# Linear attention with a beta-swish layer: where in GpSimd's queue the copy of v for batch 3 stands

## The chip, the cores and the metric

The kernel runs on one core of a Trainium2 chip. The metric is the device time of one execution in microseconds (us), as the median of several runs. Times inside an execution come from its hardware trace and count from the start of its span.

## What is computed

Two layers follow one another. First comes linear attention over 8 batches of 8 heads, 576 tokens and 64 numbers per head. Then comes a two-layer network on the 4608 tokens of 512 numbers, with a hidden width of 2048:

```python
def phi(x):                       # on q and k
    return np.where(x > 0, x, np.exp(x) - 1.0) + 1.0
kv  = np.einsum('bhsd,bhse->bhde', phi(k), v)
z   = np.sum(phi(k), axis=2)
num = np.einsum('bhsd,bhde->bhse', phi(q), kv)
den = np.einsum('bhsd,bhd->bhs', phi(q), z)[..., None] + 1e-06
x   = num / den                   # then (batch, token, head * 64)
h   = x @ w_in                    # 512 -> 2048
g   = h * (1.0 / (1.0 + np.exp(-beta * h)))
out = g @ w_out                   # 2048 -> 512
```

## The kernel before

The 576 tokens of a batch are read as 64 groups of 9. The first 8 tokens of all groups give four tiles of 128 tokens, which are the network's work of that batch, 512 tokens. The ninth tokens of all 8 batches are collected in `xT_tail` and make a ninth piece of work of the same size. So there are nine passes of the network. Each has a first half H (`h_phase`: 16 groups of 4 TensorE matmuls of 128x128 by 128x512, each followed by a swish on ScalarE, L454 and L462) and a second half Y (`y_phase`: 4 output tiles with 16 such matmuls each, L472, then a copy of the tile by VectorE, L245, and its way out by DMA). In this text, H2 and Y1 are the H half of pass 2 and the Y half of pass 1.

The attention of later batches is threaded in between. `manual_schedule` keeps every engine's instructions in the order in which the program writes them, and an engine takes its own in that order. The main loop (L838 to L871) writes pass b and keeps two lists of side work, `sh` for H and `sy` for Y: `at(sy, 5, f)` writes f behind the matmuls of group 5 of that Y half (group 4t + i is quarter i of output tile t). The number thus places the work in the queue of every engine that f uses. It is not a time: an engine that has nothing else to do takes its next instruction as soon as what it waits for is there, even when TensorE is still far from that group.

What a batch m needs, in the order of its data:

- q, k and v come by DMA. `load_q` and `load_k` are issued from GpSimd's queue, `load_v` from SyncE's for batches from 3 on. `load_q(m+1, after)` is held (`hold`, L88) until the DMA transposition of phi(q) of batch m has landed. It stands in GpSimd's queue in front of `load_k(m+2)` (L863, L864).
- phi(q) and phi(k): exp on ScalarE (L144), the positive part (L148) and a minimum (L155) on VectorE.
- phi(q) is transposed by DMA into `qTd` (L275), issued from SyncE.
- v is copied by GpSimd in two instructions (`v_copies`, L516; the copy is L173) from float32 `vf` to bfloat16 `vaug`, of which there are two, for even and odd batches. The column behind each 64 numbers of `vaug` was set to one at the start (L113), so that one matmul with phi(k) gives kv and z together.
- kv of batch m: `kv_pair` (L230) makes 36 small matmuls of 64x64 by 64x65 for half of the heads, L184. For batch 3 both halves are written in H2 by `kv_both(3)` behind group 8, right behind `odd_numers` (16 small matmuls, L356, for the ninth tokens of batches 0 and 1). For batches from 4 on they are the first matmuls of `numers` (L322) behind the last group of H.
- `numers(n, m)` makes the numerators and denominators of batch n (L309), and VectorE divides (L383 to L404). Then `x_trans_dma` (L439, issued from SyncE, L442) transposes them into `xT`, the input of H of pass n.

What stands around the change, in the pass b = 1 (n = 2, m = 3): `load_v(3)` behind group 2 of H1. In Y1, `numers(2)` behind group 1, the transpositions of batch 2's x behind groups 2 and 3, phi(q) of batch 3 behind group 3. Then:

```python
at(sy, 5, lambda: q_trans_dma(m), lambda: load_q(m + 1, st[m, "qTd", "dma"]))
at(sy, 5, lambda: load_k(m + 2))
if b == 1:
    at(sy, 8, lambda: phi_all(3, "k"), lambda: v_copies(3))
at(sy, 9, lambda: load_v(m + 1))
```

So GpSimd's queue held, in this order: the load of q of batch 3 and those of k of batches 3 and 4, the load of q of batch 4 (held), the load of k of batch 5, the copies of v of batch 3, and the copies of v of batch 4 (written in H2 behind group 6).

Of the kernel before, what the change touches and what calls it, by code (L numbers as in the profile page):

```python
# [16 lines left out]
def kernel(  # L17
# [153 lines left out]
    def v_copy(eng, b, pr):  # L171
        src = vb[b % 2] if b == 2 else vf[b % 2]
        eng.tensor_copy(  # L173
            vaug[b % 2][:, pr, :, :, 0:D], src[:, places(b, pr)].rearrange("p h j d -> p j h d")
        )
# [51 lines left out]
    def num_tile(name):  # L227
        return numps.tile([P, 2, 512], F32, tag="num", name=name)
# [4 lines left out]
    def kv_both(b):  # L233

        t = num_tile("kvp")
        for pr in range(2):
            kv_pair(b, pr, [t[:, hh, pr * EA : (pr + 1) * EA] for hh in range(2)])
        st[b, "kvd"] = work.tile([P, 2, 2 * EA], BF16, tag="kv_bd", name="kvd")
        nc.vector.tensor_copy(st[b, "kvd"], t[:, :, 0 : 2 * EA])
# [32 lines left out]
    def q_trans_dma(b):  # L272
        st[b, "qTd"] = work.tile([P, 4 * J, G], BF16, tag="qT", name="qTd")
        for hh in range(2):
            st[b, "qTd", "dma"] = nc.sync.dma_start_transpose(  # L275
                out=st[b, "qTd"][:, hh * 2 * J : (hh + 1) * 2 * J],
                in_=st[b, "q"][hh * G : (hh + 1) * G].rearrange("p a j c -> p (a j c)"),
            )

    def q_odd_trans(b, tp):  # L280

        tv = tp.rearrange("p (a n) -> p a n", a=2)
        for pr in range(2):
            nc.tensor.matmul(
                tv[:, pr], st[b, "q"][:, pr, J - 1, :], identity,
                is_transpose=True, start=True, stop=True, skip_group_check=True,
            )
        nc.scalar.copy(
            q_odd[b].rearrange("p (i a) g -> p a i g", i=2),
            tv.rearrange("p a (i g) -> p a i g", i=2),  # L290
        )
# [30 lines left out]
    def numers(b, after=None):  # L322

        pairs = [num_tile("nps") for _ in range(2)]
        odd = [mm_tile("nps_m") for _ in range(2)]
        if after is not None:
            for pr in range(2):
                kv_pair(after, pr, [pairs[pr][:, hh, 6 * EA : 7 * EA] for hh in range(2)])
        for k in range(2):
            dst = [pairs[k][:, h] for h in range(2)]  # L330
            numer_tile(b, dst, k)
            numer_tile(b, dst, 2, (k,), 4)
        numer_tile(b, odd, 3)
        for hh in range(2):
            quads(b, odd, 4 + hh, lambda c: (c, J - 1), hh, None)
        st[b, "nps"] = pairs, odd
        for k in range(3):
            norms(b, k)
        if after is not None:
            st[after, "kvd"] = work.tile([P, 2, 2 * EA], BF16, tag="kv_bd", name="kvd")  # L340
            for pr in range(2):
                nc.vector.tensor_copy(
                    st[after, "kvd"][:, :, pr * EA : (pr + 1) * EA],
                    pairs[pr][:, :, 6 * EA : 7 * EA],
                )
# [93 lines left out]
    def x_trans_dma(b, t):  # L439
        xv = st[b, "xs", t].rearrange("p n d -> p (n d)")  # L440
        if t < NT - 1:
            nc.sync.dma_start_transpose(out=x_dst(b, t), in_=xv)  # L442
            return

        for pr in range(2):
            nc.sync.dma_start_transpose(
                out=xT_tail[:, places(b, pr), b * G : (b + 1) * G],
                in_=xv[pr * G : (pr + 1) * G, 0 : 2 * P],
            )
# [39 lines left out]
    def load_q(b, after):  # L489
        if b < B:  # L490
            hold(load(nc.gpsimd, xq[b % NX], q, b), after)

    def load_k(b):
        if b < B:
            load(nc.gpsimd, xk[b % NX], k, b)

    def load_v(b):
        if b < B:
            load(nc.sync, vf[b % 2], v, b)

    def phi_exps(b, a):
        for pr in range(2):
            phi_part(b, a, pr, xin(b, a, pr))

    def phi_rest(b, a):
        phi_tile(b, a)
        for pr in range(2):
            phi_relu(b, a, pr, xin(b, a, pr))
        for pr in range(2):
            phi_min(b, a, pr)  # L510

    def phi_all(b, a):
        phi_exps(b, a)
        phi_rest(b, a)

    def v_copies(b):  # L516
        for pr in range(2):
            v_copy(nc.gpsimd, b, pr)
# [284 lines left out]
    def h_phase(b, x, side):  # L803
        for ff in range(FC):

            if b == 1 and ff in (3, 4):
                hp = num_tile("h_ps2")[:, 0]
            else:
                hp = mm_tile("h_ps")
            h_mm(b, x, ff, hp)  # L810
            silu(b, ff, hp)
            run(side, ff)

    def y_phase(b, side, last=False):
        for t in range(4):
            if last and t == 3:
                for c0, c1 in ((0, 320), (320, 512)):
                    yp = mm_tile("y_ps")
                    for i in range(4):
                        y_mm(b, t, i, yp, c0, c1)  # L820
                    y_out(b, t, yp, c0, c1, (nc.sync, nc.scalar))
                break
            yp = mm_tile("y_ps")
            halves = ((0, 256), (256, 512)) if b == 1 and t > 1 else ((0, 512),)
            for cols in halves:
                for i in range(4):
                    y_mm(b, t, i, yp, *cols)
                    if i < 3 and cols is halves[-1]:
                        run(side, 4 * t + i)
            y_out(b, t, yp)  # L830
            run(side, 4 * t + 3)

    def at(side, n, *fs):
        side.setdefault(n, []).extend(fs)
# [3 lines left out]
    for b in range(1, B + 1):  # L838
        n = b + 1
        m = n + 1  # L840
        sh, sy = {}, {}
        if b == 1:
            at(sh, 0, lambda: q_trans_dma(2))
            at(sh, 1, lambda: v_copies(2))
            at(sh, 2, lambda: load_q(3, st[2, "qTd", "dma"]), lambda: load_k(3))
            at(sh, 2, lambda: load_v(3), lambda: load_k(4))
            at(sh, 6, lambda: q_odd_trans(1, num_tile("qop")[:, 0].bitcast(BF16)[:, 0:256]))
            at(sh, 8, lambda: kv_both(2))
            at(sy, 1, lambda: numers(2))
        elif n < B:  # L850
            if b == 2:
                at(sh, 8, odd_numers, odd_norms, lambda: kv_both(3))
                at(sh, 9, lambda: [x_trans_dma(i, 4) for i in range(2)])
            if m < B:
                at(sh, 2, lambda: phi_rest(m, "k"))
                at(sh, 6, lambda: v_copies(m))
            at(sh, FC - 1, lambda: numers(n, m if m < B else None))
        if n < B:
            for t in range(NT):
                at(sy, t // 3 + (2 if b == 1 else 0), lambda t=t: x_trans_dma(n, t))  # L860
        if m < B:
            at(sy, 3, lambda: phi_all(m, "q"))
            at(sy, 5, lambda: q_trans_dma(m), lambda: load_q(m + 1, st[m, "qTd", "dma"]))  # L863
            at(sy, 5, lambda: load_k(m + 2))  # L864
            if b == 1:
                at(sy, 8, lambda: phi_all(3, "k"), lambda: v_copies(3))
            at(sy, 9, lambda: load_v(m + 1))
            if m + 1 < B:
                at(sy, 10, lambda: phi_exps(m + 1, "k"))
        h_phase(b, xT[b % 3] if b < B else xT_tail, sh)  # L870
        y_phase(b, sy, last=(b == B))  # L871
# [30 lines left out]
```

## Time and profile before

| what | before |
|---|---|
| time, median of 3 runs | 286.87 us (286.58 to 286.91) |
| span of the profiled execution | 285.2 us |
| granted TensorE clock | 0.999 |
| TensorE matmul busy | 274.3 us, 96% |
| ScalarE busy | 160.7 us, 56% |
| VectorE busy | 106.4 us, 37% |
| GpSimd busy | 37.1 us, 13% |
| DMA, mean over the span | 144 GB/s |

How to read it: PE is TensorE and PEld its loading of weights, which runs beside the matmuls; DVE is VectorE, ACT ScalarE, POOL GpSimd, SP SyncE. A q behind a name means the queue that issues (POOLq, SPq). L173 is line 173 of the kernel. A row in order of time gives the start, the duration, the engine, the line, the operation and what it wrote from what, and in square brackets how long the engine had been idle and what ended that. Matmuls overlap, so the busy time of a row is from its first start to its last end, and the ends of matmuls are modelled; intervals between starts are the better measure.

### The profile page before, as it was taken

What the parts mean: (1) busy time and instruction counts of PE and PEld (TensorE: products, weight loads), DVE (VectorE), ACT (ScalarE), POOL (GpSimd) and SP (SyncE); (2) the same over time, 40 slices, a digit from 0 to 9 for tenths busy, and PEclk for the clock granted to TensorE, in tenths of its full rate; (3) what the DMA queues carried; (4) which work ended last, traced back from release to release, by engine and by line L of the source; (5) the groups of instructions that cost most, each with busy time, mean ns of one, the idle gap of its engine ahead of it and who ended that gap; (6) DMA issues with size and microseconds to landing.
All of it is one profiled execution on the core that took longest, in us unless ns stands there. A gap on an engine that the chain in (4) does not pass through costs nothing.

```text
span 285.2 us, 5976 instructions
## 1 busy us (share of the span) xinstructions
PE 274.3 (96%) x2477; PEld 139.0 (49%) x2508; DVE 106.4 (37%) x260; ACT 160.7 (56%) x219; POOL 37.1 (13%) x51
## 2 busy tenths in 40 slices
PE   7799999999997999999999999999999999999994
PEld 2584457454844544454445444544444444444443
DVE  5842677706732464037403740281025100110012
ACT  5778587974784842885288617831860186028500
POOL 8732100320007001300041002100000000000000
PEclk9999999999999999999999999999999999999999
DMA  7999999679999928963997369336303410230033
GB/s 217 205 213 391 248 262 186 150 202 230 186 133 280 153 65 186 291 109 66 151 273 141 81 152 271 63 80 147 88 3 79 114 39 0 57 80 12 0 74 75
DMA packets 51723, 41.03 MB, mean 144 GB/s; under 512 B 31584, under 2 KB 43120, under 8 KB 51696
## 3 DMA queue, kind: packets, MB, share of 16 engines
q1 hardware_dynamic: 38800, 23.61, 35.0%
q0 software_dynamic: 12736, 16.91, 30.5%
q8 instruction: 19, 0.31, 0.5%
q10 hardware_dynamic: 160, 0.13, 0.2%
q14 instruction: 8, 0.07, 0.1%
HBM read 36.71 MB, written 9.44 MB: 162 GB/s over the span
## 4 chain that ended last, share of the span: by engine, by line
PE 90%; DMA 4%; issue 1%; ACT 1%; POOL 1%; DVE 1%; SPq 0%; POOLq 0%
PE y_ps L472 43%; PE h_ps L454 40%; DMA xk<-in_k_dram 2%; DMA qTd<-phi_q 2%; PE nps L184 1%; PE h_ps L665 1%; PE nps L309 1%; ACT e L144 1%; POOL vaug L173 1%; PE kvp L184 1%; DVE phi_k L155 1%; PE nps_m L309 0%; PE nps L631 0%; PE tp L655 0%; PE nps L563 0%
## 5 line engine op out<-in xcount | busy, mean ns | idle before, releaser
L462 ACT ACTIVATE g<-h_ps,beta_c 128x512 bf16<-128x512 f32 x144 | 97.8, 689 | 89.2 <-PE h_ps L454 88.7
L472 PE MATMUL y_ps<-w_out,g 128*128 128x512 bf16 (+3 forms) x615 | 125.9, 360 | 1.0 <-issue 0.2
L454 PE MATMUL h_ps<-xT,w_in 128*128 128x512 bf16 x487 | 108.5, 379 | 0.8 <-ACT e L144 0.3
L472 PEld LDWEIGHTS <-g 128*128 128x128 bf16 x632 | 60.8, 98 | 61.1
L454 PEld LDWEIGHTS <-w_in 128*128 128x128 bf16 x560 | 54.4, 98 | 65.6 <-DVE y_sb L245 0.7
L245 DVE COPY y_sb<-y_ps 128x512 f32<-128x512 f32 (+2 forms) x37 | 24.8, 675 | 82.5 <-PE y_ps L472 81.4
L392 DVE TENSOR_SCALAR den<-nps 128x12 f32<-128x12 f32 x12 | 2.0, 166 | 63.5 <-PE nps L309 63.5
L144 ACT ACTIVATE e<-xk 128x1152 bf16<-128x1152 bf16 x16 | 17.8, 1153 | 3.2 <-DVE phi_k L155 1.6
L83 POOL DMA_DIRECT2D xq<-in_q_dram x7 | 5.2, 746 | 95.0 <-DMA qTd<-phi_q 49.7
L144 ACT ACTIVATE e<-xq 128x1152 bf16<-128x1152 bf16 x14 | 15.6, 1155 | 1.4 <-DMA xq<-in_q_dram 1.3
L454 PE MATMUL h_ps<-xT_tail,w_in 128*128 128x512 bf16 x62 | 13.9, 379 | 0.1
L173 POOL CAST vaug<-vf 128x1152 bf16<-128x1152 f32 x10 | 11.2, 1153 | 14.3 <-DMA vf<-in_v_dram 14.3
L155 DVE TENSOR_TENSOR phi_q<-e,r 128x1152 bf16<-128x1152 bf16 (+2 forms) x17 | 11.7, 721 | 2.7 <-ACT e L144 2.4
L383 DVE TENSOR_TENSOR xs<-nps,rden 128x512 bf16<-128x512 f32 (+1 forms) x24 | 12.3, 553 | 0.4
L155 DVE TENSOR_TENSOR phi_k<-e,r 128x1152 bf16<-128x1152 bf16 x16 | 11.7, 764 | 0.3 <-ACT e L144 0.2
L144 ACT ACT_TABLE_LOAD x6 | 7.7, 1283 | 6.7 <-DMA xq<-in_q_dram 6.6
L133 PE MATMUL warm_ps<-xT 128*128 128x512 bf16 x20 | 6.5, 472 | 1.8 <-DVE xT L96 1.5
L184 PEld LDWEIGHTS <-phi_k 64*64 64x64 bf16 x576 | 5.7, 106 | 4.3 <-issue 3.7
L462 ACT ACT_TABLE_LOAD x6 | 7.7, 1283 | 0.1
L83 POOL DMA_DIRECT2D xk<-in_k_dram x9 | 6.8, 754 | 4.5 <-DMA g<-in_moe_w_out_dram 1.9
L148 DVE TENSOR_SCALAR r<-xk 128x1152 bf16<-128x1152 bf16 x16 | 7.0, 476 | 0.0
L730 DVE TENSOR_SCALAR w_out<-g,rbeta 128x512 bf16<-128x512 f32 x8 | 3.8, 536 | 8.4 <-DMA g<-in_moe_w_out_dram 8.4
(98 smaller groups left out, 118.1 us busy)
## 6 DMA issues: line engine op xcount, KB each, us to landing
out_dram<-y_sb SPq DMA_DIRECT2D x70, 128.0 KB, 2.4
vf<-in_v_dram SPq DMA_DIRECT2D x5, 1152.0 KB, 6.5
xq<-in_q_dram POOLq DMA_DIRECT2D x7, 576.0 KB, 9.5
xk<-in_k_dram POOLq DMA_DIRECT2D x7, 576.0 KB, 12.0
w_in<-in_moe_w_in_dram POOLq DMA_DIRECT2D x4, 512.0 KB, 12.3
g<-in_moe_w_out_dram POOLq DMA_DIRECT2D x2, 1024.0 KB, 17.3
stage<-in_moe_w_out_dram POOLq DMA_DIRECT2D x2, 1024.0 KB, 20.7
stage<-in_q_dram SPq DMA_DIRECT2D x2, 576.0 KB, 4.2
```

The lines of the kernel that those rows point to most:

```text
L83: return eng.dma_start(out=dst[:, h0 : h0 + n].rearrange("p h j d -> p h (j d)"), in_=rows.rearrange("(i p) e -> p i e", p=P)[:, h0 : h0 + n],
L133: nc.tensor.matmul(warm_ps[:, 0:cols], warm[:, 0:P], warm[:, 0:cols], start=True, stop=True)
L144: nc.scalar.activation(st[b, a, pr, "e"][:, :, j0:j1], x[:, :, j0:j1], ACTF.Exp)
L148: nc.vector.tensor_scalar(r, x, 0.0, 1.0, ALU.max, ALU.add)
L155: nc.vector.tensor_tensor(st[b, a][:, pr, j0:j1].rearrange("p j (h d) -> p j h d", h=2), st[b, a, pr, "e"][:, :, j0:j1].rearrange("p h j d ...
L173: eng.tensor_copy(vaug[b % 2][:, pr, :, :, 0:D], src[:, places(b, pr)].rearrange("p h j d -> p j h d"))
L184: nc.tensor.matmul(dst[hh][c], st[b, "k"][r, pr, j, c], mov(r, j, h), start=(j == 0), stop=(j == J - 1), skip_group_check=True,)
L245: eng.tensor_copy(dst, src)
L383: nc.vector.tensor_mul(out, num, rd[..., None].to_broadcast(list(num.shape)))
L454: nc.tensor.matmul(hp[:, c0:c1], w_in_sb[ff // 4][:, kc, (ff % 4) * P : (ff % 4 + 1) * P], x[:, kc, c0:c1], start=(kc == 0), stop=(kc == K ...
L462: nc.scalar.activation(g_sb[b % 2][:, ff, :], hp, ACTF.Silu, scale=beta_c[:, ff : ff + 1])
L472: nc.tensor.matmul(yp[:, c0:c1], g_sb[b % 2][:, ff, t * P : (t + 1) * P], w_out_sb[i][:, c, c0:c1], start=(ff == 0), stop=(ff == FC - 1), ...
```

## The change

The copies of v of batch 3 were written behind group 8 of Y1, and are written behind group 4. That puts them in front of the held load of q of batch 4 in GpSimd's queue, and leaves phi(k) of batch 3 where it was.

```diff
             at(sy, 5, lambda: q_trans_dma(m), lambda: load_q(m + 1, st[m, "qTd", "dma"]))
             at(sy, 5, lambda: load_k(m + 2))
             if b == 1:
-                at(sy, 8, lambda: phi_all(3, "k"), lambda: v_copies(3))
+                at(sy, 4, lambda: v_copies(3))
+                at(sy, 8, lambda: phi_all(3, "k"))
             at(sy, 9, lambda: load_v(m + 1))
```

The instructions are the same, in the same number. What it is for: the copies no longer stand behind a load that waits for phi(q) of batch 3 to be transposed, so that vaug of batch 3 is ready before `kv_both(3)` asks for it.

## The prediction

> **What bounds the kernel now.** I read the page first (TensorE busy 96% of the span, granted clock 0.999), then the waits of TensorE from 50 us on, then the chain that ended last around the wait found there, then the instructions in order of time on both sides of it.
>
> TensorE sets the end. Its waits between 50 and 282 us are short to list (columns: who waited for whom, us in total, times, longest):
>
> ```profile
> PE kvp L184 <- POOL vaug L173: 1.4, 2, 0.8
> PE y_ps L472 <- issue: 0.2, 1, 0.2
> ```
>
> So after 50 us TensorE waits for another engine in one place only, and it is the place of the change: kv of batch 3 waits for GpSimd's two copies. The chain that ended last, in order of time (start, us, what), tells why they were late:
>
> ```profile
> 66.67 12.13 PE y_ps L472 x87
> 78.80 0.33 SPq L275
> 79.13 0.04 issue
> 79.17 5.18 DMA qTd<-phi_q
> ...
> 84.89 0.09 POOL xq L83
> 84.98 0.64 issue
> 85.62 0.75 POOL xk L83
> 86.37 2.25 POOL vaug L173 x2
> 88.62 0.04 issue
> 88.66 0.48 PE kvp L184 x36
> ```
>
> The transposition of phi(q) lands at 84.36, releases the held load of q, the load of k follows, and only then come the copies. Behind 89 us the chain is TensorE alone to 281.6 us, so a microsecond gained here is one at the end, unless something else comes to wait. TensorE at that place, in order of time:
>
> ```profile
> 86.48 0.32 PE L356 MATMUL nps_o<-kv,q_odd 64*64 64x65 bf16 x16
> 87.57 0.48 PE L184 MATMUL kvp<-vaug,phi_k 64*64 64x65 bf16 x36 [0.77 <-POOL vaug L173]
> 88.66 0.48 PE L184 MATMUL kvp<-vaug,phi_k 64*64 64x65 bf16 x36 [0.61 <-POOL vaug L173]
> 89.07 1.25 PE L454 MATMUL h_ps<-xT,w_in 128*128 128x512 bf16 x4
> ```
>
> GpSimd, in order of time:
>
> ```profile
> 63.22 1.50 POOL L83 DMA_DIRECT2D xk<-in_k_dram  x2
> 84.89 0.75 POOL L83 DMA_DIRECT2D xq<-in_q_dram  x1 [20.18 <-DMA qTd<-phi_q]
> 85.62 0.75 POOL L83 DMA_DIRECT2D xk<-in_k_dram  x1
> 86.36 2.25 POOL L173 CAST vaug<-vf 128x1152 bf16<-128x1152 f32 x2
> 90.50 2.25 POOL L173 CAST vaug<-vf 128x1152 bf16<-128x1152 f32 x2 [1.89 <-DMA vf<-in_v_dram]
> ```
>
> From 64.72 to 84.89 GpSimd stands idle before the held load, with the copies behind it.
>
> **What the Trainium skill says.** "TensorE: Matmul & The Clock Gate", section on the array's architectural detail, calls GpSimd's queue strictly first in, first out. The trace agrees: 20.18 us idle before the held load, though v of batch 3 had been asked for at 59.84. "SBUF — State Buffer", section "Who interferes with whom", says that VectorE and GpSimd share a pair of ports as an exclusive lock: VectorE in a two-port mode, or with two SBUF inputs against a GpSimd instruction that reads SBUF, blocks or is blocked for the whole instruction; with at most one SBUF input and outside those modes it does not contend. That matters, since the copies move beside other VectorE work. What the trace says follows below.
>
> **The change part by part.**
>
> *Removed: the wait of kv of batch 3.* The load of v (L83, SyncE) is issued at 59.84 and its time to landing in that window is 5.8 us, so v is there at 65.6. GpSimd has finished its loads at 64.72. The copies then start at about 65.8 (in the row at 90.50 the start came 0.17 after the landing, 83.73 + 6.6 = 90.33) and take 2.25 us: vaug of batch 3 is ready at 68.1, some 18 us before TensorE asks. phi(k) of batch 3, the other input, is ready at 81.6 (L155, 80.16 + 1.42), so it does not take the wait's place. Then TensorE runs on from `odd_numers`. The price of 72 such matmuls without a wait comes from batch 2's kv: first start 57.09, next H matmul 57.83, so 0.74 us or 10.3 ns each. From 86.48: 16 x 10.3 ns = 0.16, 72 x 10.3 ns = 0.74, so the next H matmul starts at 87.38 in place of 89.07. Gain 1.69 us. The two idle times alone, 0.77 + 0.61 = 1.38 us, are the lower bound: they leave out that each row's end is drawn out by the modelled end of its last matmul, about 0.19 us. I take 1.69, since it is measured from start to start.
>
> *Moved: 2.25 us of GpSimd work from 86.4 to 65.8.* It hides in the 20.18 us of idle time. The held load of q of batch 4 stands behind it, but waits until 84.36 in any case, so it and the load of k of batch 5 are issued as before, at 84.89 and 85.62. Nothing is later.
>
> *Copies beside VectorE's divisions.* From 66.15 to 70.6 VectorE divides for batch 2, in the kernel's tightest place: SyncE transposes the results one after the other, the last of the four with 4.5 us to landing from 73.58, hence 78.1, and TensorE wants them for H2 at 78.6. Slack 0.5 us. But before, the same three kinds of operation (denominator, reciprocal, product with an input in PSUM) ran beside the same copies:
>
> ```profile
> 86.86 0.17 DVE L368 TENSOR_SCALAR den<-nps_o 128x8 f32<-128x8 f32 x1 [5.28 <-PE nps_o L356]
> 87.06 0.20 DVE L369 RECIPROCAL rden<-den 128x8 f32<-128x8 f32 x1
> 87.30 0.76 DVE L383 TENSOR_TENSOR xs<-nps_o,rden 128x256 bf16<-128x256 f32 x2
> ```
>
> Start to start these are 0.20 and 0.24 us; without a copy beside them, at 66.15, 66.35 and 66.61, they are 0.20 and 0.26. No block, as the page on SBUF has it for one SBUF input. Cost 0. The copies end before the two-port candidates on bfloat16 (L148 at 71.14) begin.
>
> *What comes 1.69 us earlier and may meet something that doesn't.* (a) v of batch 4 lands at 90.3 as before and its copies end at 92.75. Its matmuls come at 95.22 - 1.69 = 93.53: slack 0.8 us. (b) q of batch 4 is issued at 84.89 with 11.3 us to landing: 96.2. ScalarE, free at about 94.3, waits 1.9 us for it, but its exps and table load end at 103.9 as before and its next swish is at 111.50 - 1.69 = 109.8. Hidden by 5.9 us. (c) VectorE and SyncE behind the divisions of batch 3 move with TensorE. The four tail transpositions end at 92.8, before the first of batch 3 would come (97.50 - 1.69 = 95.8). (d) In the later passes the copies end 3.8 us or more ahead (120.5 against 124.34) and all of it moves together. Cost 0 each.
>
> Sum: 286.87 - 1.69 = 285.18 us.
>
> **The rivals.**
>
> *A: the next copies take over the wait.* If v of batch 4 lands later, or its copies are slower, by 1.4 us, the slack of 0.8 is used up and 0.6 us comes back: 285.8. For it: landings of such loads vary (5.8 and 6.6 us in two passes). Against: neither their issue nor their company in the queues changes.
>
> *B: the copies hold VectorE.* If its divisions wait for both copies, they start at 68.1 and not 66.15, 1.9 us late; the transpositions land at 80.0 and H2 starts 1.9 - 0.5 = 1.4 us late. Net -1.69 + 1.4 = -0.3: 286.6, no change that a measurement tells. For it: the port lock, and a slack of only 0.5. Against: the rows at 86.86 to 87.30.
>
> *C: slower.* B, and the copies also hold up the loads of k that GpSimd issued at 63.22 to 64.72, by their 2.25 us. The exps of k (72.16, 75.99) and the table load behind them then end about 2.25 us later, and the first swish of H2 ends at 80.37 + 2.25 = 82.6, while TensorE wants its buffer for the fifth group at 78.62 + 4 x 0.865 = 82.1. Adding that 0.5 and an equal loss in the next exchange of buffers to B: 286.6 + 1.0 = 287.6. For it: GpSimd issues those loads. Against: all three issues are over 1 us before the copies start.
>
> **How the numbers follow.** Forecast 0.80, A 0.10, B 0.06, C 0.04. The predicted time is the forecast's, 285.2. Its own bounds are 1.38 us (285.5) and 1.69 with the 0.16 us by which the runs before lie about their middle (285.0); two tenths more below for the spread of another measurement give 284.8. Above, the range takes in A, 285.8, with a tenth for that spread: 285.9. B and C are left out, 0.10. The bound of 0.2% is 0.57 us, so faster is below 286.3: forecast and A, 0.90, less 0.01 for a smaller gain: 0.89. Same is B and that 0.01: 0.07. Slower is C: 0.04.
>
> **What would show it.** In the profile after: GpSimd's copies for batch 3 at 65.8 behind the loads of k; no line of TensorE waiting for vaug; the first H matmul behind kv of batch 3 at 87.4; the load of q of batch 4 still at about 84.9; den at 66.15, 66.35 and 66.61 unmoved; H2 starting at 78.6; the copies for batch 4 at 90.5, and no wait of their matmuls at 93.5. Wrong would be: a wait for vaug near 93.5 (A), VectorE's reciprocal or products starting only behind the copies and TensorE idle before 78.6 (B), ScalarE's exps of k starting late (C), or a landing of v well behind 65.6, which would put the copies beside the two-port work at 71.

## The result, and the profile after

| | before | after |
|---|---|---|
| time, median | 286.89 us (286.58 to 287.55, 4 runs) | 285.42 us (285.10 to 285.77, 4 runs) |
| ratio after / before, 95% interval | | 0.9946 [0.9924, 0.9968] |
| span of the profiled execution | 285.2 us | 283.3 us |

The forecast was 285.2 us, in a range of 284.8 to 285.9. The change gained 1.5 us here. Two repetitions, told below, gave 0.9 and 0.8 us, and much of what follows is about that difference.

TensorE's waits between 50 and 282 us (who waited for whom, us in total, times, longest) are down to one line. The line that had vaug in it is gone:

```profile
PE y_ps L472 <- issue: 0.2, 1, 0.2
```

GpSimd after, in order of time (start, us, engine, line, operation):

```profile
63.21 1.49 POOL L83 DMA_DIRECT2D xk<-in_k_dram  x2
65.72 2.24 POOL L173 CAST vaug<-vf 128x1152 bf16<-128x1152 f32 x2 [1.02 <-DMA vf<-in_v_dram]
83.80 0.75 POOL L83 DMA_DIRECT2D xq<-in_q_dram  x1 [15.84 <-DMA qTd<-phi_q]
84.53 0.76 POOL L83 DMA_DIRECT2D xk<-in_k_dram  x1
89.44 2.24 POOL L173 CAST vaug<-vf 128x1152 bf16<-128x1152 f32 x2 [4.15 <-DMA vf<-in_v_dram]
```

The copies stand where the working put them (65.8 forecast, 65.72 measured), ahead of the held load, which still waits for the transposition of phi(q). TensorE after, at the same place:

```profile
78.38 7.93 PE L454 MATMUL h_ps<-xT,w_in 128*128 128x512 bf16 x35
86.25 0.32 PE L356 MATMUL nps_o<-kv,q_odd 64*64 64x65 bf16 x16
86.40 0.81 PE L184 MATMUL kvp<-vaug,phi_k 64*64 64x65 bf16 x72
87.14 6.22 PE L454 MATMUL h_ps<-xT,w_in 128*128 128x512 bf16 x27
```

The 72 matmuls of kv are one row without a gap. From the first of `odd_numers` to the next H matmul there are 87.14 - 86.25 = 0.89 us, where the kernel before took 89.07 - 86.48 = 2.59: 1.70 us less (forecast: 1.69). H2 itself began 0.24 us earlier in this execution (78.38 against 78.62), which is no part of the change: TensorE was ahead by as much before Y1's output matmuls went on (numerators of batch 2 at 65.47 against 65.70). The two together are the difference of the spans, 1.9 us.

### The profile page after: what moved, and what is told of

Read it like the earlier page. It is cut to its first block, busy times and chain, and to the rows that moved or that the text cites. A ratio compares the mean times of both kernels' runs of the same rounds, so it can differ in the third digit from the quotient of the medians.

```text
span 283.3 us, 5976 instructions
## 1 busy us (share of the span) xinstructions
PE 274.6 (97%) x2477; PEld 139.0 (49%) x2508; DVE 106.1 (37%) x260; ACT 160.5 (57%) x219; POOL 37.2 (13%) x51
## 4 chain that ended last, share of the span: by engine, by line
PE 81%; DMA 13%; POOL 2%; ACT 1%; issue 1%; DVE 0%; POOLq 0%; ACTq 0%
PE y_ps L472 39%; PE h_ps L454 39%; DMA xq<-in_q_dram 8%; DMA w_in<-in_moe_w_in_dram 5%; PE nps L184 1%; POOL w_in L120 1%; PE nps L309 1%; ACT e L144 1%; POOL vf L83 1%; ACT xT L435 1%; PE kvp L184 0%; PE nps_m L309 0%; POOL xk L83 0%; DVE y_sb L245 0%; POOL identity masks.py:199 0%
## 5 line engine op out<-in xcount | busy, mean ns | idle before, releaser
L133 PE MATMUL warm_ps<-xT 128*128 128x512 bf16 x20 | 7.3, 516 | 1.8 <-DVE xT L96 1.5
```

What stands on the lines that cost most here:

```text
L133: nc.tensor.matmul(warm_ps[:, 0:cols], warm[:, 0:P], warm[:, 0:cols], start=True, stop=True)
```

## The experiments

My theory was that the wait of kv for vaug is the whole effect. The rivals were that it matters where the copies run, and that the moved copies can hold up VectorE. All kernels do the full computation; `e_dve_late` repeats some of it. Measured times:

| run | median, us (runs) | before beside it | ratio, 95% interval |
|---|---|---|---|
| r_after | 285.98 (22) | 286.88 | 0.998 [0.9963, 0.9996] |
| e_between | 286.36 (22) | 286.88 | 0.9985 [0.9973, 0.9996] |
| e_late_kv | 287.96 (22) | 286.88 | 1.0044 [1.0026, 1.0063] |
| e_no_hold | 294.31 (5) | 286.88 | 1.0256 [1.023, 1.0281] |
| e_xt_after | 285.68 (22) | 287.05 | 0.9958 [0.9943, 0.9973] |
| e_xt_before | 286.64 (14) | 287.05 | 1.0002 [0.9975, 1.0028] |
| e_after_kv11 | 287.50 (22) | 287.05 | 1.0025 [1.0007, 1.0043] |
| e_dve_late | 287.25 (13) | 287.05 | 1.0008 [0.9997, 1.0018] |
| r_before2 | 286.39 (1) | 286.79 | |
| r_after2 | 286.01 (22) | 286.79 | 0.9979 [0.996, 0.9997] |
| e_xt_after2 | 285.41 (20) | 286.79 | 0.9947 [0.9931, 0.9964] |
| e_port | 286.16 (10) | 286.79 | 0.9986 [0.9962, 1.0011] |

Kernels of one block (lines 1 to 4, 5 to 8, 9 to 12) ran on one chip and share the runs of the kernel before.

### The changed kernel again

> The changed kernel again, for the size of the gain beside the runs below. The theory (all of the gain is TensorE's wait for vaug of batch 3, 1.7 us from start to start): 1.4 to 1.7 us below the kernel before. If part of the gain were a matter of the day: clearly less.

The gain was 0.90 us between the medians, less than expected, and the interval of the ratio reaches from almost nothing to 1.1 us. As in the first profile after, TensorE has no wait for vaug. Perhaps the 1.69 us that the first profile shows is not what the wait usually costs.

### Copies between the two loads

```diff
             at(sy, 5, lambda: q_trans_dma(m), lambda: load_q(m + 1, st[m, "qTd", "dma"]))
+            if b == 1:
+                at(sy, 5, lambda: v_copies(3))
             at(sy, 5, lambda: load_k(m + 2))
             if b == 1:
-                at(sy, 8, lambda: phi_all(3, "k"), lambda: v_copies(3))
+                at(sy, 8, lambda: phi_all(3, "k"))
```

> The kernel before with the copies of v of batch 3 between the held load of q of batch 4 and the load of k of batch 5. The theory: they start at about 85.6 and not 86.4, kv's second half at about 87.95 and not 88.66, the H matmul behind it at 88.35 and not 89.07: 0.7 us below the kernel before, with TensorE's wait for vaug down from 1.4 to about 0.7 us. The load of k of batch 5 is issued 2.25 us later, its exps too, hidden on ScalarE. The rival (what counts is where the copies run, away from the loads, the divisions and kv at 84 to 89 us, not how long TensorE waits): no gain, since they still run there.

0.5 us gained between the medians (forecast 0.7), with the copies still at 85.3 us. The rival of the place, which forecast no gain, has the interval against it, though only just. But the profile did not look as I had expected:

```profile
79.48 7.93 PE L454 MATMUL h_ps<-xT,w_in 128*128 128x512 bf16 x35 [0.53 <-issue]
87.34 0.32 PE L356 MATMUL nps_o<-kv,q_odd 64*64 64x65 bf16 x16
87.49 0.81 PE L184 MATMUL kvp<-vaug,phi_k 64*64 64x65 bf16 x72
```

No wait for vaug at all. TensorE came to kv 0.9 us later than in the first profile, because H2 began at 79.48 and not at 78.62. The copies were ready by then. This is the first sign that the length of the wait depends on when H2 begins.

### kv later, with the copies where they were and where they are now

```diff
-                at(sh, 8, odd_numers, odd_norms, lambda: kv_both(3))
+                at(sh, 8, odd_numers, odd_norms)
+                at(sh, 11, lambda: kv_both(3))
```

> The kernel before, its copies untouched, but kv of batch 3 is written three groups of H2 later, behind group 11. The theory: TensorE comes there at about 89.2, the copies have been ready since 88.6, no wait is left, and the time is that of the changed kernel, 1.4 to 1.7 us below the kernel before. The rival (the late copies cost by where they run): no gain, or less than half of it.

The wait for vaug went, as forecast, and the time rose by 1.1 us, which neither side forecast. The rows of TensorE show a new pause among the numerators of batch 3:

```profile
89.83 0.93 PE L184 MATMUL kvp<-vaug,phi_k 64*64 64x65 bf16 x72
90.69 3.63 PE L454 MATMUL h_ps<-xT,w_in 128*128 128x512 bf16 x15
94.25 0.81 PE L184 MATMUL nps<-vaug,phi_k 64*64 64x65 bf16 x72
94.87 0.45 PE L309 MATMUL nps<-kvd,qTd 64*64 64x65 bf16 x32
96.52 0.32 PE L309 MATMUL nps<-kvd,qTd 64*64 64x65 bf16 x16 [1.20 <-issue]
```

The pause comes after 32 of the 72 numerator matmuls, and "issue" says that no wait on another engine accounts for it. To see whose it is, the same edit was made to the changed kernel.

> The changed kernel with kv of batch 3 behind group 11 of H2 and not group 8. Nobody waits for vaug in either place. The theory (the late kv without waits lost its gain to the place of the kv matmuls themselves, a pause of 1.2 us among the numerators of batch 3 behind it, and not to where the copies run): this kernel has the same pause and lies 1 to 2 us above the changed kernel, like the earlier run with late kv. The rival (the late copies on GpSimd cost the time): no pause, time as the changed kernel, 286.0.

```profile
95.19 0.45 PE L309 MATMUL nps<-kvd,qTd 64*64 64x65 bf16 x32
97.55 0.32 PE L309 MATMUL nps<-kvd,qTd 64*64 64x65 bf16 x16 [1.90 <-issue]
```

The pause is there again, after the same 32 matmuls, with the copies done since 68.7 us. So it belongs to the late place of kv and not to the late copies, and the two kernels with the late kv lie above the kernel before by like amounts (1.0044 and 1.0025, overlapping intervals). What makes the pause stays open. Two dense blocks of small matmuls stand closer together than before, which would suit a shortage of instructions, but the trace shows no late fetch of them, so this is not shown. As a test of the theory this pair is half a success: removing the wait by waiting elsewhere worked, and cost more than it brought.

### The load not held

```diff
-            hold(load(nc.gpsimd, xq[b % NX], q, b), after)
+            d = load(nc.gpsimd, xq[b % NX], q, b)
+            if b != 4:
+                hold(d, after)
```

> The kernel before with the order of GpSimd's queue untouched, but the load of q of batch 4 is not held. The theory: loads of q and k at 64.7 to 66.2, copies at 66.2 to 68.5, no wait for vaug; but 1.15 MB of loads now run beside the transpositions of batch 2's x, which have 0.5 us of slack. If they land later by x, H2 starts x - 0.5 late: I expect x of 1 to 3 us and a time of 285.7 to 287.7. The rival (the hold protects nothing): as the changed kernel, 285.4.

The transpositions were late, as the theory had it, but by far more, and the time rose by 7.4 us, outside the forecast. The copies ran at 67.2 and nothing waited for vaug, but:

```profile
85.80 0.58 PE L454 MATMUL h_ps<-xT,w_in 128*128 128x512 bf16 x1 [6.52 <-DMA xT<-xs]
86.60 9.57 PE L454 MATMUL h_ps<-xT,w_in 128*128 128x512 bf16 x34 [0.22 <-issue]
96.10 0.32 PE L356 MATMUL nps_o<-kv,q_odd 64*64 64x65 bf16 x16
```

Beside the extra loads the last three transpositions of batch 2's x took 11.1 to 14.2 us to land; with the hold they took 4.5 to 7.8. H2 began 7.2 us late. And after an idle time of 6.5 us the granted clock was 0.50 from 85.8 to 90 us, so that H2 up to `odd_numers` took 10.3 us (96.10 - 85.80) in place of 7.9. "TensorE: Matmul & The Clock Gate" of the Trainium skill, section "Part 1: The HAM clock gate", describes just this: half the clock after an idle window, and the full one back after some us of work. The hold earns its wait: without it the loads cost more than the wait for vaug. The copies had to be taken out from behind it, not it from before them.

### The start of H2

`e_between` pointed to the start of H2. It needs the four transpositions of batch 2's x; between the third and the fourth stand two output transfers in SyncE's queue. This edit takes them out of the way, in the changed kernel and in the kernel before:

```diff
-                at(sy, t // 3 + (2 if b == 1 else 0), lambda t=t: x_trans_dma(n, t))
+                at(sy, 2 + t // 4 if b == 1 else t // 3, lambda t=t: x_trans_dma(n, t))
```

> The changed kernel, with the fourth transposition of batch 2's x issued right behind the third, ahead of the first two output transfers (1.2 us of SyncE's queue). The theory (TensorE's start of H2 hangs on that transposition's landing, 78.1 to 79.4 in the runs so far, where TensorE is free at about 78.4; the kernel before hides such a lateness in its wait for vaug, the changed one does not, which is why its gain came out as 0.9 us in place of 1.5 on this day): the landing comes about 1 us earlier, H2 starts at 78.4 without a wait, and the median falls to 285.3, with fewer runs far above it. The rival (the transposition is never late; the runs far above the median have another cause): as the changed kernel, 286.0.

285.68 us on one chip. Since no changed kernel ran beside it there, it was run once more with one:

> The changed kernel with the earlier fourth transposition once more, on one chip with the changed kernel. The theory: it takes away the wait of 0 to 0.6 us at the start of H2 and so gains 0.2 to 0.4 us over the changed kernel. The rival: no difference.

> The changed kernel a third time, beside the next one. The theory: the mean of the wait that it removes, some 1.3 us, so 0.9 to 1.5 us below the kernel before; in the profile the H matmul behind kv starts 8.8 us after H2 starts, whatever the held load does.

On one chip: 285.41 us (285.18 to 286.10) against 286.01 us (285.54 to 288.85). The move gains 0.6 us over the changed kernel, more than the 0.2 to 0.4 forecast, and the intervals of the two ratios overlap by 0.0004 only. The changed kernel itself lies 0.78 us below the kernel before here, short of the 0.9 to 1.5 forecast. The start of H2 in the changed kernel and then with the fourth transposition moved:

```profile
79.20 7.93 PE L454 MATMUL h_ps<-xT,w_in 128*128 128x512 bf16 x35 [0.47 <-issue]
```

```profile
78.58 7.93 PE L454 MATMUL h_ps<-xT,w_in 128*128 128x512 bf16 x35
```

The "issue" wait is the transposition. In `r_after2` the fourth goes out at 73.76 and takes 5.3 us to landing, hence 79.06, and H2 starts at 79.20. In `r_before2`: 73.13 + 6.2 = 79.33, start 79.45. In `e_between`: 73.52 + 5.9 = 79.42, start 79.48. In `r_after`: 73.50 + 5.1 = 78.60, start 78.70. Only in the two profiles that I compared first, before (78.1) and after (73.33 + 4.8 = 78.13), was TensorE itself the later one, at 78.62 and 78.38. With the transposition moved (`e_xt_after2`) it lands at 72.4 + 5.8 = 78.2, and H2 starts at 78.58 without a wait.

The runs far above the median are another matter. On this chip the moved transposition had none (highest 286.10 us), but on the chip of `e_xt_after` it had (285.15 to 287.94). The profile of `e_xt_after` fell on the highest of these: the granted clock was 0.50 from 13 to 19 us, TensorE came to the numerators of batch 2 at 68.35 (65.66 in `e_xt_after2`), and H2 started without a wait. Those 2.5 us were lost early in the kernel. For that run the rival was right: it has another cause than the transposition.

> The kernel before with the same move of the fourth transposition. The theory: H2 starts on time, but TensorE then waits for vaug all the same, so the time stays within 0.3 us of the kernel before (286.9), and the difference to the changed kernel with the same move is the whole 1.5 to 1.7 us. The rival (transposition and copies are two separate costs that add): it gains as much here as it does on the changed kernel.

Inconclusive: 286.64 against 287.05 us, with an interval of the ratio from 0.9975 to 1.0028 and single runs from 285.55 to 290.09. My theory said that the wait for vaug would stay. It mostly went in this profile, which fell on the fastest of the 14 runs: the transposition of phi(q), next in the same queue, also left earlier, and the held load went out at 83.43. The two effects can't be taken apart this way. What the pair gives is the worth of the copies' move with H2 on time on one chip: 286.64 - 285.68 = 0.96 us, and not the 1.5 to 1.7 forecast.

### The wait again

> The kernel before again, for a second profile of its wait. The theory by now: the wait is not a fixed 1.7 us. It is the difference of two times that both hang on DMA landings and vary from execution to execution: the held load of q of batch 4 goes out at t (83.4 to 86.0 in the profiles so far) and the H matmul behind kv can start at t + 4.2; TensorE, without the wait, would be there 8.8 us after the start of H2 (78.4 to 79.5). So here that matmul starts at t + 4.2 if this is later than the start of H2 + 8.8, and the wait is the difference of the two, between 0 and 2.4 us. The rival (a fixed wait): 1.4 us of waiting for vaug again.

The kernel before, a second profile, TensorE and then GpSimd:

```profile
79.45 7.93 PE L454 MATMUL h_ps<-xT,w_in 128*128 128x512 bf16 x35 [0.80 <-issue]
87.31 0.32 PE L356 MATMUL nps_o<-kv,q_odd 64*64 64x65 bf16 x16
87.47 0.99 PE L184 MATMUL kvp<-vaug,phi_k 64*64 64x65 bf16 x72
88.39 6.22 PE L454 MATMUL h_ps<-xT,w_in 128*128 128x512 bf16 x27
```

```profile
84.20 0.74 POOL L83 DMA_DIRECT2D xq<-in_q_dram  x1 [19.17 <-DMA qTd<-phi_q]
84.93 0.76 POOL L83 DMA_DIRECT2D xk<-in_k_dram  x1
85.67 2.26 POOL L173 CAST vaug<-vf 128x1152 bf16<-128x1152 f32 x2
```

In this execution of the unchanged kernel there was next to nothing to gain. The held load goes out at 84.20, so the H matmul behind kv can start at 84.20 + 4.18 = 88.38 (4.18 = 89.07 - 84.89 of the first profile). It starts at 88.39. Without the wait TensorE would have been there 8.76 us after the start of H2 (87.14 - 78.38 of the changed kernel; 8.75 to 8.89 in the eight profiles at full clock in which kv stood in its old place and did not wait): 79.45 + 8.76 = 88.21. The wait was 0.17 us and not 1.69, give or take the 0.1 us by which the 8.76 varies. A fixed wait is refuted.

The same sum can be done for each profile whose queues are alike up to the held load. Only the rows of before and `r_before2` are waits that took place. The other six are estimates of what the copies would have cost with copies and kv in their old places:

| profile | held load out | + 4.18 | H2 starts | + 8.76 | wait |
|---|---|---|---|---|---|
| before | 84.89 | 89.07 | 78.62 | 87.38 | 1.69 |
| r_before2 | 84.20 | 88.38 | 79.45 | 88.21 | 0.17 |
| after | 83.80 | 87.98 | 78.38 | 87.14 | 0.84 |
| r_after | 84.87 | 89.05 | 78.70 | 87.46 | 1.59 |
| r_after2 | 84.77 | 88.95 | 79.20 | 87.96 | 0.99 |
| e_between | 84.60 | 88.78 | 79.48 | 88.24 | 0.54 |
| e_late_kv | 86.02 | 90.20 | 79.03 | 87.79 | 2.41 |
| e_after_kv11 | 85.12 | 89.30 | 79.43 | 88.19 | 1.11 |

The mean is 1.17 us. The late start of H2 works against the wait: it is time in which the held load and the copies catch up. The three measurements of the change gave 1.47, 0.90 and 0.78 us between the medians, mean 1.05.

### Had the copies held VectorE

```diff
-            scale(x, nv[:, :, 0:4, 0:D], rden[:, :, 0:4])
+            for _ in range(5 if (b, k) == (2, 0) else 1):
+                scale(x, nv[:, :, 0:4, 0:D], rden[:, :, 0:4])
```

> The changed kernel with the first product of batch 2's divisions repeated four times on VectorE, 4 x 0.47 = 1.9 us more in front of the transpositions: what it would have cost had the moved copies held VectorE for their whole length. The theory: the fourth transposition lands at about 80.0 and not 78.1, H2 starts at about 79.9 to 80.2 and not 78.4 to 78.7, and the time rises by 1.4 to 1.9 us over the changed kernel. The rival (there is slack of 2 us or more there, so that the divisions don't matter): no change.

The expected mechanism was wrong, and the size too. The four extra products took longer than the 1.9 us on which the forecast rests. VectorE in the changed kernel and then here:

```profile
66.39 1.02 DVE L383 TENSOR_TENSOR xs<-nps,rden 128x512 bf16<-128x512 f32 x2
```

```profile
66.82 3.92 DVE L383 TENSOR_TENSOR xs<-nps,rden 128x512 bf16<-128x512 f32 x6
```

That is 3.92 - 1.02 = 2.90 us of delay, and still the cost was smaller than forecast. The median lies 0.20 us above the kernel before beside it, so about 1.0 to 1.1 us above the changed kernel, if that lay 0.8 to 0.9 below as in its two repetitions; forecast were 1.4 to 1.9. H2 started at 80.59, later than forecast, but not for a transposition: the fourth landed at 75.66 + 2.5 = 78.2.

```profile
66.65 5.35 PE L473 MATMUL y_ps<-w_out,g 128*128 128x512 bf16 x24
73.59 5.63 PE L473 MATMUL y_ps<-w_out,g 128*128 128x256 bf16 x50 [1.58 <-DVE xs_odd L383]
```

TensorE stopped in Y1 already, until VectorE's last division of batch 2. That division frees the tiles of the numerators in PSUM (the memory that TensorE writes its results to), which share a pool of four with the output tiles. VectorE came 2.90 us later and TensorE lost 1.58, so the slack for VectorE, by this one profile, is about 1.3 us, and it lies there. A delay of 1.9 us, what copies that hold VectorE for their whole length would cause, would then cost about 0.6 us (an estimate, 1.9 - 1.3) and not 1.4 to 1.9. With H2 no longer held up by a transposition, the median less that wait, 287.25 - 1.58 = 285.67, also fits the kernel with the moved transposition on the same chip, 285.68.

The last experiment puts the moved copies beside other work of VectorE (a part of the edit; `d` is the copy of `v_copy`, and the rest of it keeps the exps for `hold` to name):

```diff
+        if b == 3:
+            hold(d, st[3, "q", 0, "exp"])
```

> The changed kernel, with the moved copies held until the first exp of phi(q) of batch 3 is done, at about 71.0. There VectorE works on bfloat16 in SBUF alone (positive part, then a minimum of two inputs), and no longer with an input in PSUM as beside the divisions. The theory (VectorE and GpSimd block each other over the shared ports for such operations, and the changed kernel's copies were free of it only by what runs beside them): the copies or these VectorE rows become longer by 0.5 us or more, or start late, and the time stays as the changed kernel, since phi(q) has over 4 us until its transposition. The rival (no such block in this kernel at all): copies 1.12 us each from start to start, rows of 0.41 and 0.71 us as before.

VectorE in the changed kernel, two instructions to a row:

```profile
70.91 0.82 DVE L148 TENSOR_SCALAR r<-xq 128x1152 bf16<-128x1152 bf16 x2
71.64 1.42 DVE L155 TENSOR_TENSOR phi_q<-e,r 128x1152 bf16<-128x1152 bf16 x2
```

With the copies held, VectorE and GpSimd together, one instruction to a row:

```profile
71.41 0.45 DVE L150 TENSOR_SCALAR r<-xq 128x1152 bf16<-128x1152 bf16 x1
71.46 1.41 POOL L175 CAST vaug<-vf 128x1152 bf16<-128x1152 f32 x1 [6.31 <-ACT e L144]
71.78 1.70 DVE L157 TENSOR_TENSOR phi_q<-e,r 128x1152 bf16<-128x1152 bf16 x1
72.82 1.67 POOL L175 CAST vaug<-vf 128x1152 bf16<-128x1152 f32 x1
73.40 1.69 DVE L157 TENSOR_TENSOR phi_q<-e,r 128x1152 bf16<-128x1152 bf16 x1
```

The two minima with both inputs in SBUF went from 1.42 to 3.31 us together, and the copies from 2.24 to 3.02. The theory of contention holds, and the time shows nothing of it (286.16 us against 286.01), since phi(q) had time to spare. Each minimum took 1.7 us in place of 0.75, and each copy 1.41 or 1.67 in place of 1.15. They overlap in the rows, but the order of the ends shows turns: the second positive part ends at 71.86, the first copy 1.01 us later, the first minimum 0.61 after that, the second copy 1.01 after that, the second minimum 0.60 after that. So each ends a fixed time after the other engine's last one, a little less than it takes alone. Had the two engines shared the ports evenly, the second minimum would not have had 0.60 of its 0.75 us left when the second copy ended, 1.09 us after it had begun. This is what an exclusive lock does, and the trace agrees with the Trainium skill ("SBUF — State Buffer", "Who interferes with whom"). The positive part, which the prediction named as a two-port candidate, seems to have held the first copy in the same way. The changed kernel's copies run beside divisions with an input in PSUM, and neither side is longer there.

## Why the prediction was right, and what it mis-sized

- *The wait and its cause.* Right. kv waited for copies that stood in a first-in-first-out queue behind a held load; with the copies ahead the wait is gone.
- *The 1.69 us.* Right for the execution from which it was worked out (1.70 in the profile after), and too large as a typical value. That the first measurement (1.47 us) came so near it is in part luck. This is the mis-sized term. It took the difference of two times in one profile as a constant, and both hang on DMA landings. Over eight profiles (two measured, six estimated) it lies between 0.17 and 2.41 us with a mean of 1.17. The forecast of 285.2 us was 0.2 under the first measurement and 0.8 under the two repetitions, which lie just above the range. Their gains, by ratios of 0.998 and 0.9979, are at the bound of 0.2%. All three intervals hold the ratios from 0.9963 to 0.9968, a gain of 0.9 to 1.1 us. The 1.38 us that the prediction took as a lower bound was none either.
- *Copies beside the divisions cost 0.* Right: den, reciprocal and the first product at 65.92, 66.12 and 66.39 keep the distances 0.20 and 0.27 us beside the copies. The slack that I named there was wrong. VectorE's own is some 1.3 us, through the PSUM tiles (an estimate from `e_dve_late`). Rival B, which reckoned with 0.5, was therefore priced too high: by that estimate it would have cost about 0.6 us and not 1.4. The 0.5 us of the fourth transposition belonged to that execution; in the four other profiles listed above the landing is what H2 waits for. What the prediction says of the lock, that the later one waits, came out in `e_port`.
- *Held load and load of k as before.* Right: 83.80 and 84.53, a little earlier, since phi(q)'s transposition landed earlier.
- *(a) the next copies.* Right: they end at 91.7, their matmuls begin at 93.29. Rival A did not come.
- *(b) ScalarE's wait for q of batch 4.* Right: 1.04 us of idle time at 95.12, and the table load behind the exps starts at 101.55, long before the next swish.
- *(c) VectorE moves with TensorE.* Wrong, without harm. A new wait came, which I had not worked out:

```profile
97.44 0.23 DVE L404 RECIPROCAL rden<-den 128x12 f32<-128x12 f32 x1
99.54 0.76 DVE L383 TENSOR_TENSOR xs<-nps_m,rden 128x256 bf16<-128x256 f32 x2 [1.87 <-DMA xT_tail<-xs]
101.01 0.68 DVE L245 COPY y_sb<-y_ps 128x512 f32<-128x512 f32 x1
```

  I had compared the times at which SyncE issues. What matters is that the division writes a buffer that the tail transposition of batches 0 and 1 still reads until it lands. VectorE was back on its old time (copy at 101.01, before 101.11), which was early enough for TensorE.
- *Rivals B and C.* Neither came. VectorE's rows kept their distances and the exps of k were not late (71.91 and 75.91).

## What to carry to other kernels

When an engine waits for something behind a held instruction in a first-in-first-out queue, move the work out from behind the hold, and ask what the hold protects before loosening it: here that cost 7.4 us. A wait read from one profile is the difference of two moving times. If either hangs on a DMA landing, take it from several profiles before calling it the gain. And when one wait goes, look for the next in line: a transposition issued ahead of two output transfers took off another 0.6 us on the chip where both ran, at 285.4 us.

## What the runs showed of the hardware that was not expected

- 1.15 MB of loads put beside four DMA transpositions took the landing of the last three from 4.5 to 7.8 us to 11.1 to 14.2 us.
- VectorE minima with both inputs in SBUF and GpSimd copies written at the same time took turns: each copy ended 1.01 us, each minimum 0.60 to 0.61 us after the end of the other engine's last instruction, though the profile's rows overlap. In such rows the duration (1.7 us for a minimum of 0.75) contains the waiting.
- TensorE paused 1.20 and 1.90 us within a run of 64x64 matmuls, twice after the same 32, with no wait that the trace shows.
